# Scores of the first two head pairs taken in row halves of the array from the split halves

## The chip, the cores and the metric

One core of a Trainium2 chip runs the whole program in one launch. The metric is device time in microseconds, the median of several executions; the profile shows one further execution. TensorE (PE) multiplies, with PEld its weight loads; VectorE (DVE), ScalarE (ACT) and GpSimd (POOL) work beside it, and SyncE (SP) issues most DMAs, in the order of its queue. Every engine works through its own instructions in order.

## The reference

Inputs are q, k, v of 2 batches x 8 heads x 768 positions x 64 dimensions, in fp32. Attention is masked by a hash: six projections give six sign bits to each position, and a query sees the keys that have its six bits.

```python
q_bits = (np.einsum('bhsd,dk->bhsk', q, proj) > 0)      # six bits, the same for k
mask = q_bucket[:, :, :, None] == k_bucket[:, :, None, :]
scores = np.where(mask, scale * np.matmul(q, k.transpose(0, 1, 3, 2)), -1e9)
attn = np.exp(scores - np.max(scores, axis=-1, keepdims=True))
attn = attn / (np.sum(attn, axis=-1, keepdims=True) + 1e-09)
return np.matmul(attn, v)
```

The result, 768 x 512 for each batch, goes through a mixture of eight experts with one expert for each token (a gate decides whether a token keeps the expert of the one before it), and then through a second mixing layer over tokens and channels. Both follow the attention, and the change does not touch them.

## The kernel before

The attention walks over eight head pairs (a batch and two neighbouring heads); a pair's q and k lie transposed in one tile `rqk`, with head 0 in partitions 0 to 63 and head 1 in 64 to 127. A **unit** is one head and 128 queries of a pair against all 768 keys, so a pair has 12 units and there are 96; three query blocks of both heads, six units, are a group. The kernel keeps fp32 accuracy with single-pass products: every number is split into a high part (rounded) and a low part (the rest), and the scores are high x high + high x low + low x high. The mask is added by the same matmuls: 12 rows of bits (six signs and their complements, k's scaled by 2^31) add a huge number where a bit differs.

To make three products and the bits with two matmuls of 128 and 76 rows, the parts of a head are first **placed**: `split_hi` and `split_lo` (lines 139 to 162) make the tile `hl` with q high, q low, k high, k low; `place` (L164 to 179) copies them by DMA into `op`, where head h has four operands: q high twice one above the other, k high above k low, q low above q's bits, and k high above k's bits. Pair 0's head 0 is placed by ScalarE, POOL and VectorE at the start instead (L421 to 436). The bits come from `bit_dots` (L109), which uses the array in four column quarters, and `bit_signs`.

Per unit u: `scores` (L187) writes 128 x 768 scores into `ps`, of which there are two; `low` (L202, VectorE, printed at L205) copies them into `sc` and takes their minimum; `expo` (L209, ScalarE) takes the exponential and the sum; `transp` (L215) turns `sc` by six TensorE transposes into two tiles `pst`, evacuates them (two of two on ScalarE for units in `relieve`, otherwise one on ScalarE and one on VectorE), and issues `low` and `expo` of unit u + 2 in between. `av` (L238) multiplies with v, both heads in column halves, one group late; `av_out` and `av_tok` finish a group. The instructions of VectorE's `low` at L205 stand in the order of units, so the n-th of them is that of unit n - 1.

The main loop (L456 on) issues, for each u: `scores(u + 2)`, for odd u of a later group `av`, `transp(u)`, token work of earlier groups, and then what a table `todo` holds for u. That table is filled by `at(u, f)`: the splits and placements of pair n during pair n - 1 (three units later for pair 1), loads of later pairs and of v, bit steps, and single pieces of work for the later layers (`narrow`, errands). So SP's queue holds placements and loads in the order of their units, and each waits for its source.

Of the kernel before, what the change touches and what calls it, by code (L numbers as in the profile page):

```python
# [24 lines left out]
CAP = 256  # L25
OVF = E * CAP
NOV = 64
NW = 4
C_ID, C_TRI, C_ONE = 0, 128, 256
C_CODE, C_M0, C_TOK, C_IOTA, C_W = 128, 136, 142, 154, 410  # L30
THR = -1.5 * 2.0 ** -23
# [22 lines left out]
def warm(nc, cbf, ps, n):  # L54
    for _ in range(n):
        nc.tensor.matmul(ps[:, :384], lhsT=cbf[:, 0:128], rhs=cbf, start=True, stop=True)


def attention(tc, nc, cst, cbf, cst_src, tri_src, cw, qkT, vt, iw_src, route, wide, errands, xh, early):
    with ExitStack() as ctx:  # L60
# [21 lines left out]

        pairs = [(b, p) for b in range(B) for p in range(NP)]
        NPR = len(pairs)
        rawt, vtile, bits, opnd, hls = {}, {}, {}, {}, {}

        def load_pair(i):
            b, p = pairs[i]
            r = raw_p.tile([128, 2, S], F32, name="rqk")
            if i == 0:  # L90
                nc.sync.dma_start(r[:, 1], qkT[b, p, :, 1])
                nc.sync.dma_start(r[:, 0], qkT[b, p, :, 0])
# [39 lines left out]
        def bits_here(s, hf, pd):  # L132
            sl, p = slice(384 * hf, 384 * hf + 384), 64 * s
            to = opnd[0][64:76, 0, 2 + s, sl]
            nc.vector.tensor_scalar(to, pd[p:p + 12, :384], 0.0, cw[p:p + 12, 32:33],
                                    op0=ALU.is_gt, op1=ALU.subtract)
            return to

        def split_hi(i, j):
            raw = rawt[i]  # L140
            if j == 0:
                hls[i] = hl_p.tile([128, 4, S], F32R, name="hl")
                if i == 0:
                    nc.scalar.activation(hls[i][:, 2], raw[:, 1], AF.Copy)
                else:
                    nc.gpsimd.tensor_scalar(hls[i][:, 2], raw[:, 1], 1.0, 0.0, op0=ALU.mult, op1=ALU.add)
            elif i == 0:
                nc.scalar.activation(hls[i][:, 0], raw[:, 0], AF.Copy, scale=-0.125)
            else:
                nc.gpsimd.tensor_scalar(raw[:, 0], raw[:, 0], -0.125, 0.0, op0=ALU.mult, op1=ALU.add)  # L150
                nc.gpsimd.tensor_scalar(hls[i][:, 0], raw[:, 0], 1.0, 0.0, op0=ALU.mult, op1=ALU.add)

        def split_lo(i, j):
            raw, hl = rawt[i], hls[i]
            if j == 0:
                eng = nc.gpsimd if i else nc.vector
                eng.tensor_tensor(hl[:, 3], raw[:, 1], hl[:, 2].bitcast(F32), op=ALU.subtract)
            elif i == 0:
                nc.vector.scalar_tensor_tensor(hl[:, 1], raw[:, 0], -0.125, hl[:, 0].bitcast(F32),
                                               op0=ALU.mult, op1=ALU.subtract)  # L160
            else:
                nc.gpsimd.tensor_tensor(hl[:, 1], raw[:, 0], hl[:, 0].bitcast(F32), op=ALU.subtract)

        def place(i, h, j):  # L164
            if i not in opnd:
# [19 lines left out]
        pss, scs, pts, sums, mns, pav, xTs = {}, {}, {}, {}, {}, {}, {}  # L185

        def scores(u):  # L187
            i, half, qb, h = units[u]
# [26 lines left out]
        def transp(u):  # L215
            _, _, qb, h = units[u]
            g = u // 6
            if u % 6 == 0:
                pts[g] = [pt_p.tile([128, NB, 384], F32, name=f"pt{x}") for x in range(2)]
            sc = scs.pop(u)  # L220
            pt = pts[g][h]
            for n in range(2):
                ps = ps_t.tile([128, 512], F32, name="pst")
                for j in range(3):
                    kb = 3 * n + j
                    nc.tensor.transpose(ps[:, 128 * j:128 * j + 128], sc[:, 128 * kb:128 * kb + 128], ident)  # L226
# [8 lines left out]
            if u + 2 < NU:  # L235
                expo(u + 2)

        def av(g, kb, q0=0, q1=3):  # L238
# [114 lines left out]
        def at(u, f, *args):  # L353
            todo[u].append(lambda: f(*args))

        busy, relieve = set(), set(range(1, NU - 1, 2))
        for n in range(1, NPR):
            u0 = 12 * (n - 1)
            u1 = u0 + 3 if n == 1 else u0
            at(u1, split_hi, n, 0)  # L360
            at(u1, split_hi, n, 1)
            at(u1 + 1, split_lo, n, 0)
            at(u1 + 2, split_lo, n, 1)
            for h in range(2):
                for j in range(4):
                    at(u1 + 3 + j, place, n, h, j)
            if n + 3 < NPR:
                at(u1 + 8, load_pair, n + 3)
            if n + 1 < NPR:
                at(u1 + 8, load_v, n + 1)  # L370
        for u0, ids in ((1, [1]), (9, [2, 3]), (26, [4, 5]), (50, [6, 7])):
            for hf in range(2):
                at(u0 + hf, lambda ids=ids, hf=hf: bit_part(ids, hf, px_tile))
                busy.add(u0 + hf)
# [37 lines left out]
        load_pair(0)  # L412
        nc.sync.dma_start(cst, cst_src)
        load_pair(1)
        idle = ps_a.tile([128, 512], F32, name="pav")
        warm(nc, cbf, idle, 13)
        opnd[0] = op_p.tile([128, 2, 4, S], F32R, name="op")
        op = opnd[0]
        split_hi(0, 0)
        hl = hls[0]  # L420
        split_lo(0, 0)  # L421
        split_hi(0, 1)
        for x in (1, 3):
            nc.gpsimd.tensor_scalar(op[0:64, 0, x], hl[0:64, 2], 1.0, 0.0, op0=ALU.mult, op1=ALU.add)
        pds = [bit_dots([0], hf, pt_tile) for hf in range(2)]
        warm(nc, cbf, idle, 6)
        split_lo(0, 1)
        nc.scalar.activation(op[0:64, 0, 0], hl[0:64, 0], AF.Copy)
        nc.scalar.activation(op[64:128, 0, 1], hl[0:64, 3], AF.Copy)
        nc.scalar.activation(op[64:128, 0, 0], hl[0:64, 0], AF.Copy)  # L430
        nc.scalar.activation(op[0:64, 0, 2], hl[0:64, 1], AF.Copy)
        k0 = bits_here(1, 0, pds[0])
        bits_here(0, 0, pds[0])
        nc.vector.tensor_scalar(k0, k0.bitcast(F32), -MISS, None, op0=ALU.mult)
        k1 = bits_here(1, 1, pds[1])
        nc.vector.tensor_scalar(k1, k1.bitcast(F32), -MISS, None, op0=ALU.mult)
        place(0, 1, 0)
        place(0, 1, 1)
        place(0, 1, 2)
        for hf in range(2):  # L440
            bit_signs(bits[0][0], hf, pds[hf])
        place(0, 1, 3)
        nc.sync.dma_start(op.bitcast(F32)[64:76, 0, 2, 384:], bits[0][0][0:12, 384:])
        nc.sync.dma_start(iw, iw_src)
        nc.sync.dma_start(tri, tri_src)
        load_v(0)
        load_pair(2)
        load_v(1)
        load_pair(3)
        for u in range(2):  # L450
# [5 lines left out]
        for u in range(NU):  # L456
            g, w = u // 6, u % 6
            last = g == NG - 1
            if u + 2 < NU:
# [887 lines left out]
def build(tc, nc, a):  # L1347
    with ExitStack() as ctx:
# [6 lines left out]
        cw = P.tile([128, 33], F32, name="cw")  # L1355
# [75 lines left out]
def arrange(inp):  # L1431
# [1 line left out]

    c = np.ascontiguousarray
    cst, tri = consts()
    cw = np.zeros((128, 33), np.float32)
# [4 lines left out]
    cw[:, 32] = np.where(np.arange(128) < 64, ~first, first)  # L1441
    out = {"cst": cst, "tri": tri, "cw": cw}
    qk = np.stack([inp["q"], inp["k"]], axis=3)
    out["qkT"] = c(np.transpose(qk, (0, 1, 4, 3, 2))).reshape(B, NP, 128, 2, S)
# [28 lines left out]
```

## Time and profile before

| | us |
|---|---|
| median of three runs | 642.21 (639.51 to 643.21) |
| the profiled execution | 639.75 |
| its span, first to last instruction | 637.9 |
| TensorE busy in the span | 621.0 |
| start of the first unit's `low` | 11.60 |
| start of the `low` of unit 24 | 70.52 |

A row of the timeline gives start, length, engine, line, operation, result<-operands, partitions x columns, count; neighbouring instructions of one kind are merged, and the brackets say how long the engine sat idle before and what ended it. The length of a matmul contains its way through the array, so neighbours overlap: a stream's cost is the distance of starts.

### The profile page before, as it was taken

How to read it: one execution, taken by the hardware profiler on the slowest of the kernel's cores; microseconds unless marked ns; L12 is line 12 of the kernel's file. 1: busy time of each engine (PE TensorE's matmuls, PEld its weight loads, DVE VectorE, ACT ScalarE, POOL GpSimd, SP SyncE). 2: the span in 40 equal slices, each digit the busy share in tenths (PEclk: the TensorE clock that was granted, in tenths of full speed). 3: DMA queues.
4: the chain of work that ended last, by engine and by line, in shares of the span. 5: the costliest groups of instructions: out<-in, count | busy, mean ns of one | idle time of the engine just before them, and what ended most of it. 6: DMA issues, size and time to landing. Idle time of an engine off the chain costs nothing. (4 is left out here: it accounts for less than half of the span.)

```text
span 637.9 us, 10353 instructions
## 1 busy us (share of the span) xinstructions
PE 621.0 (97%) x3930; PEld 501.9 (79%) x3930; DVE 404.0 (63%) x743; ACT 355.3 (56%) x645; POOL 262.0 (41%) x195
## 2 busy tenths in 40 slices
PE   7989998999999999999999999999999999999997
PEld 4746766667677677889899889989688887878897
DVE  6636768788888666846885655644356877663352
ACT  5747766767767766454555455444656546743220
POOL 2432221124080241345346354255456766684320
PEclk8979999999999999999999999999999999999999
DMA  7997999965976201688768698764222432221002
GB/s 198 265 234 203 305 260 289 260 165 159 259 219 157 74 1 50 232 294 316 272 226 312 233 308 306 256 247 168 82 85 85 145 100 84 101 97 67 33 34 100
DMA packets 52861, 116.13 MB, mean 182 GB/s; under 512 B 4180, under 2 KB 13664, under 8 KB 52808
## 3 DMA queue, kind: packets, MB, share of 16 engines
q1 hardware_dynamic: 49448, 101.28, 51.2%
q10 hardware_dynamic: 1440, 7.86, 3.6%
q0 software_dynamic: 1920, 6.29, 3.0%
q8 instruction: 32, 0.52, 0.3%
q14 instruction: 21, 0.17, 0.1%
HBM read 74.06 MB, written 22.54 MB: 151 GB/s over the span
## 5 line engine op out<-in xcount | busy, mean ns | idle before, releaser
L205 DVE TENSOR_SCALAR_CACHE_REDUCE sc<-ps 128x768 f32<-128x768 f32 x96 | 91.4, 953 | 33.2 <-PE ps L198 32.2
L1199 PE MATMUL acc<-wt,z 128*128 128x256 f32 (+1 forms) x576 | 105.4, 338 | 0.6 <-DVE z L1185 0.6
L1199 PEld LDWEIGHTS acc<-wt,z 128*128 128x128 f32 x576 | 89.8, 188 | 15.7 <-DVE z L1185 1.5
L784 POOL TENSOR_TENSOR whl<-wr,whl 128x1024 fp32r<-128x1024 f32 x30 | 72.0, 2425 | 69.6 <-ACT whl L782 69.6
L212 ACT ACTIVATE sc<-sc,mn 128x768 f32<-128x768 f32 x96 | 89.8, 936 | 18.6 <-DVE sc L205 15.4
L198 PE MATMUL ps<-op 76*128 76x384 f32 (+1 forms) x384 | 94.2, 367 | 4.8 <-DMA op<-bt 2.2
L857 PE MATMUL mph<-xhl,whl 128*128 128x256 f32 x768 | 94.2, 284 | 0.4 <-DVE xhl L520 0.3
L857 PEld LDWEIGHTS mph<-xhl,whl 128*128 128x128 f32 x768 | 93.2, 192 | 1.3 <-DVE xhl L520 0.5
L226 PEld LDWEIGHTS pst<-cst,sc 128*128 128x128 f32 x576 | 66.5, 143 | 31.7 <-ACT sc L212 18.5
L230 ACT ACTIVATE pt<-pst 128x384 f32<-128x384 f32 x143 | 65.0, 487 | 41.8 <-PE pst L226 41.5
L226 PE MATMUL pst<-cst,sc 128*128 128x128 f32 x576 | 83.6, 282 | 1.7 <-DVE pt L232 1.6
L873 PE MATMUL mpy<-whl,h 128*128 128x512 f32 x336 | 79.5, 392 | 0.0
L198 PEld LDWEIGHTS ps<-op 76*128 76x128 f32 (+1 forms) x384 | 64.5, 194 | 12.9 <-issue 5.9
L243 PE MATMUL pav<-pt,v 128*64 128x384 f32 (+1 forms) x432 | 74.2, 468 | 0.0
L782 ACT ACTIVATE whl<-wr 128x1024 fp32r<-128x1024 f32 x64 | 64.0, 1051 | 15.1 <-PE mpy L873 6.5
L873 PEld LDWEIGHTS mpy<-whl,h 128*128 128x128 f32 x336 | 62.1, 188 | 12.4
L552 POOL TENSOR_TENSOR wt<-wr,wt 128x768 fp32r<-128x768 f32 x24 | 46.2, 1946 | 10.0 <-ACT wt L551 4.6
L243 PEld LDWEIGHTS pav<-pt,v 128*64 128x64 f32 x432 | 26.4, 137 | 28.7 <-issue 28.5
L784 DVE TENSOR_TENSOR whl<-wr,whl 128x1024 fp32r<-128x1024 f32 x34 | 40.0, 1219 | 6.4 <-ACT whl L782 6.4
L860 ACT ACTIVATE h<-mph 128x512 fp32r<-128x512 f32 x32 | 19.1, 596 | 43.1 <-PE mph L857 41.6
L861 DVE SCALAR_TENSOR_TENSOR h<-mph,h 128x512 fp32r<-128x512 f32 x32 | 21.8, 689 | 33.3 <-ACT h L860 33.2
L1225 PE MATMUL bk<-u,wch 128*128 128x512 f32 (+1 forms) x192 | 34.0, 335 | 0.9 <-DVE u L1215 0.9
(186 smaller groups left out, 792.7 us busy)
## 6 DMA issues: line engine op xcount, KB each, us to landing
wr<-w SPq DMA_DIRECT2D x32, 1024.0 KB
op<-hl SPq DMA_DIRECT2D x45, 384.0 KB
wr<-wtf ACTq DMA_DIRECT2D x10, 768.0 KB
w<-wt SPq DMA_DIRECT2D x16, 384.0 KB
rqk<-qkT SPq DMA_DIRECT2D x7, 768.0 KB
xs<-wr SPq DMA_DIRECT2D x8, 512.0 KB
xi<-xs SPq DMA_DIRECT2D x7, 512.0 KB
ys<-y SPq DMA_DIRECT2D x7, 512.0 KB
```

Source lines behind the costliest of these rows:

```text
L198: nc.tensor.matmul(ps[:, n, :384], lhsT=op[:kk, h, x, c0:c0 + 128], rhs=op[:kk, h, x + 1, 384 * n:384 * n + 384], start=(x == 0), stop=(x ...
L205: nc.vector.tensor_scalar(sc.rearrange("p (a b) -> p a b", a=2), pss.pop(u)[:, :, :384], NEG, None, op0=ALU.min, op1=ALU.min, accum_out=mn ...
L212: nc.scalar.activation(sc, sc, AF.Exp, bias=mns[g][:, w:w + 1], scale=-1.0, accum_out=sums[g][:, w:w + 1])
L226: nc.tensor.transpose(ps[:, 128 * j:128 * j + 128], sc[:, 128 * kb:128 * kb + 128], ident)
L230: nc.scalar.activation(dst, src, AF.Copy)
L243: nc.tensor.matmul(pav[g][64 * h:64 * h + 64, sl], lhsT=vtile[g // 2][:, kb, 64 * h:64 * h + 64], rhs=pts[g][h][:, kb, sl], start=(kb == 0 ...
L552: self.nc.gpsimd.tensor_tensor(t[:, 1, r], raw[:, sl], t[:, 0, r].bitcast(F32), op=ALU.subtract)
L782: nc.scalar.activation(t[0][:, sl], raw[:, sl], AF.Copy)
L784: lo.tensor_tensor(t[1][:, sl], raw[:, sl], t[0][:, sl].bitcast(F32), op=ALU.subtract)
L857: nc.tensor.matmul(ps[:, ff], lhsT=w[a][:, w0:w0 + 128], rhs=x[:, bb, k], start=(n == 0), stop=(n == 23))
L873: nc.tensor.matmul(yps[e][n], lhsT=h[:, a, fo, 128 * n:128 * n + 128], rhs=w[bb][:, 512 * f:512 * f + 512], start=(fo == 0 and q == 0), st ...
L1199: nc.tensor.matmul(span(b, d, t0, n), lhsT=z[:, a, r, 128 * d:128 * d + 128], rhs=w[:, bb, r, t0:t0 + n], start=(t == 0 and i == 0 and (d ...
```

## The change

For pairs 0 and 1 (24 units) nothing is placed. `scores2` takes the scores of both heads of one query block in one set of sixteen matmuls, from `hl` where it is: three products, two halves of the keys, two heads, each with 64 rows; head 0 uses rows 0 to 63 of the array and head 1 rows 64 to 127. The bits follow as four matmuls of 12 rows that begin at rows 0, 32, 64 and 96, from tiles that hold every bit row at the place it is used from. It takes both `ps` tiles at once. The loop goes over such sets for the first 22 units; units 22 on run in the old loop. For an odd unit `transp` now issues `low(u + 2)` ahead of its first evacuation and `expo(u + 2)` ahead of its second.

Pair 0's bits are made at their places by three steps with a whole 128-partition result (`first_dots`, `first_signs`); its q is loaded and split in two halves, so that the first set needs only the first. Pair 1's bits are made as before and spread by 12 small DMAs (`second_bits`), eight after unit 5 and four after unit 8; its splits on POOL come after units 0 and 4. The constants, v and the third pair are loaded ahead of the first computing. Six warm-up matmuls go. Both `hl` lie in what was the first operand tile, and the bits in the tile of the expert stage's tokens, which is free then.

```diff
+        def first_dots(x, alloc):
+            pd = alloc()
+            for r in range(4):
+                c, w0 = 32 * r, 12 * (r // 2)
+                rhs = rawt[0][:, 1, HALF[r % 2]] if x == 2 else rawt[0][:, 0, HALF[x]]
+                nc.tensor.matmul(pd[c:c + 32, :384], lhsT=cw[:, w0:w0 + 32], rhs=rhs,
+                                 start=True, stop=True, tile_position=(0, c))
+            return pd
+
+        def first_signs(x, pd):
+            q, k = bbs[0]
+            to, c = (k, 34) if x == 2 else (q[x], 33)
+            nc.vector.tensor_scalar(to, pd[:, :384], 0.0, cw[:, c:c + 1], op0=ALU.is_gt, op1=ALU.subtract)
+            if x == 2:
+                nc.scalar.activation(to, to.bitcast(F32), AF.Copy, scale=-MISS)
...
+        def second_bits(x):
+            bt, r0 = bits[1]
+            q, k = bbs[1]
+            for h in range(2):
+                c = r0 + 12 * h
+                for n in range(2):
+                    r = slice(64 * h + 32 * n, 64 * h + 32 * n + 12)
+                    if x == 0:
+                        nc.sync.dma_start(k.bitcast(F32)[r], bt[64 + c:76 + c, HALF[n]])
+                    nc.sync.dma_start(q[x].bitcast(F32)[r], bt[c:c + 12, HALF[x]])
...
-        units[:6] = sorted(units[:6], key=lambda t: (t[3], t[2]))
...
+        NP2 = 24
+
+        def scores2(p):
+            i, half, qb, _ = units[2 * p]
+            hl, g = hls[i], p // 3
+            q, k = bbs[i]
...
+            ps = [ps_s.tile([128, 2, 512], F32, name="ps") for _ in range(2)]
+            c0 = 384 * half + 128 * qb
+            cols = slice(c0, c0 + 128)
+            for x, (a, bc) in enumerate(((0, 2), (0, 3), (1, 2))):
+                for n in range(2):
+                    for h in range(2):
+                        hs = slice(64 * h, 64 * h + 64)
+                        nc.tensor.matmul(ps[h][:, n, :384], lhsT=hl[hs, a, cols], rhs=hl[hs, bc, HALF[n]],
+                                         start=(x == 0), stop=False)
+            for n in range(2):
+                for h in range(2):
+                    r = slice(64 * h + 32 * n, 64 * h + 32 * n + 12)
+                    nc.tensor.matmul(ps[h][:, n, :384], lhsT=q[half][r, 128 * qb:128 * qb + 128], rhs=k[r],
+                                     start=False, stop=True)
...
+                if u < NP2 - 2 and h == 1:
+                    if n == 0:
+                        low(u + 2)
+                        nc.vector.tensor_copy(dst, src)
+                    else:
+                        expo(u + 2)
+                        nc.scalar.activation(dst, src, AF.Copy)
+                    continue
...
+        busy, relieve = set(), set(range(0, NP2 - 2, 2)) | set(range(NP2 - 1, NU - 1, 2))
         for n in range(1, NPR):
             u0 = 12 * (n - 1)
+            at(u0, split_hi, n, 0)
+            if n == 1:
+                at(u0, split_lo, n, 0)
+                at(u0 + 4, split_hi, n, 1)
+                at(u0 + 4, split_lo, n, 1)
+                at(u0 + 5, second_bits, 0)
+                at(u0 + 8, second_bits, 1)
...
+        nc.scalar.activation(hl[:, 2], rawt[0][:, 1], AF.Copy)
+        first_hi(0)
+        pd = first_dots(2, pt_tile)
+        nc.vector.tensor_tensor(hl[:, 3], rawt[0][:, 1], hl[:, 2].bitcast(F32), op=ALU.subtract)
+        first_signs(2, pd)
+        pd = first_dots(0, pt_tile)
+        first_lo(0)
+        first_signs(0, pd)
+        scores2(0)
+        pd = first_dots(1, px_tile)
         for u in range(2):
-            scores(u)
             low(u)
             expo(u)
+        first_signs(1, pd)
+        at(0, first_hi, 1)
+        at(1, first_lo, 1)
...
+        for p in range(NP2 // 2 - 1):
+            g, w = p // 3, p % 3
+            scores2(p + 1)
+            transp(2 * p)
+            if g >= 1:
+                av(g - 1, 2 * w)
+                av(g - 1, 2 * w + 1)
+                if w == 2:
+                    av_out(g - 1)
+            transp(2 * p + 1)
+            for u in (2 * p, 2 * p + 1):
+                for x in tok.get(u, ()):
+                    av_tok(x)
+                for f in todo.pop(u, ()):
+                    f()
+        for u in range(NP2 - 2, NU):
```

## Rows read from the trace of the kernel before

**Rows 1.** The page: busy time, share of the span and instructions of each engine.

```profile
PE 621.0 (97%) x3930; PEld 501.9 (79%) x3930; DVE 404.0 (63%) x743; ACT 355.3 (56%) x645; POOL 262.0 (41%) x195
```

**Rows 2.** Busy time by stretch; columns: stretch, length, each engine, clock, DMA share, GB/s.

```profile
5.30:12.10 6.80, 4.95 (x32) 2.31 (x30) 6.55 (x10) 4.13 (x6) 3.86 (x4) 1.00 0.96 252
12.10:19.00 6.90, 6.39 (x28) 5.09 (x28) 3.82 (x9) 4.71 (x10) 0.93 (x3) 0.51 0.72 181
39.40:46.30 6.90, 6.90 (x27) 3.12 (x26) 2.95 (x8) 1.97 (x5) 4.26 (x5) 0.51 0.81 241
```

**Rows 3.** TensorE's waits, 70.5 to 637 us, longest first: total, times, longest.

```profile
PE pst L226 <- DVE pt L232: 1.6, 1, 1.6
```

**Rows 4.** The start, in order of time: start us, length us, engine, line, operation.

```profile
5.35 0.96 DVE L157 TENSOR_TENSOR hl<-rqk,hl 128x768 fp32r<-128x768 f32 x1 [4.10 <-ACT hl L144]
5.53 1.50 PE L118 MATMUL pst<-rqk,cw 128*32 128x384 f32 x16
11.60 0.95 DVE L205 TENSOR_SCALAR_CACHE_REDUCE sc<-ps 128x768 f32<-128x768 f32 x1
12.47 0.95 DVE L205 TENSOR_SCALAR_CACHE_REDUCE sc<-ps 128x768 f32<-128x768 f32 x1
```

**Rows 5.** The timeline around pair 1's first unit.

```profile
34.67 0.85 PE L118 MATMUL px<-rqk,cw 128*32 128x384 f32 x8
35.65 0.62 DVE L125 TENSOR_SCALAR bt<-px,cw 128x384 f32<-128x384 f32 x1 [2.06 <-issue]
38.31 0.30 PEld L198 LDWEIGHTS ps<-op 76*128 76x128 f32 x2 [2.56 <-DMA op<-bt]
39.52 1.51 PE L118 MATMUL px<-rqk,cw 128*32 128x384 f32 x8
```

**Rows 6.** The timeline of one round with `av`; narrow windows split some merged rows.

```profile
53.69 1.51 PE L243 MATMUL pav<-pt,v 128*64 128x384 f32 x8
54.39 0.82 PE L243 MATMUL pav<-pt,v 128*64 128x384 f32 x4
54.71 0.49 PE L243 MATMUL pav<-pt,v 128*64 128x384 f32 x2
55.13 0.88 PE L226 MATMUL pst<-cst,sc 128*128 128x128 f32 x6
55.76 0.95 PE L198 MATMUL ps<-op 128*128 128x384 f32 x4
56.38 0.34 PE L198 MATMUL ps<-op 76*128 76x384 f32 x1
56.55 0.82 PE L226 MATMUL pst<-cst,sc 128*128 128x128 f32 x6
56.84 0.96 DVE L205 TENSOR_SCALAR_CACHE_REDUCE sc<-ps 128x768 f32<-128x768 f32 x1 [1.98 <-PE ps L198]
57.13 0.95 PE L198 MATMUL ps<-op 128*128 128x384 f32 x4
58.01 1.51 PE L243 MATMUL pav<-pt,v 128*64 128x384 f32 x8
```

**Rows 7.** The timeline: `low` of units 5, 8, 9 and 24.

```profile
22.71 0.96 DVE L205 TENSOR_SCALAR_CACHE_REDUCE sc<-ps 128x768 f32<-128x768 f32 x1 [0.32 <-PE ps L198]
26.95 0.96 DVE L205 TENSOR_SCALAR_CACHE_REDUCE sc<-ps 128x768 f32<-128x768 f32 x1 [0.56 <-ACT pt L230]
28.31 0.96 DVE L205 TENSOR_SCALAR_CACHE_REDUCE sc<-ps 128x768 f32<-128x768 f32 x1
70.52 0.96 DVE L205 TENSOR_SCALAR_CACHE_REDUCE sc<-ps 128x768 f32<-128x768 f32 x1 [0.56 <-PE ps L198]
```

**Rows 8.** The timeline: one bit DMA's issue; first and last step of pair 1's split.

```profile
13.54 0.72 SPq L443 DMA_DIRECT2D op<-bt  x1
23.07 0.83 POOL L146 TENSOR_SCALAR hl<-rqk 128x768 fp32r<-128x768 f32 x1
27.37 1.84 POOL L162 TENSOR_TENSOR hl<-rqk,hl 128x768 fp32r<-128x768 f32 x1
```

More of the change, by code (lines that the diff above doesn't have):

```diff
@@ L28 @@
 NW = 4
+HALF = slice(0, 384), slice(384, 768)
 C_ID, C_TRI, C_ONE = 0, 128, 256
@@ L84, in attention @@
         NPR = len(pairs)
-        rawt, vtile, bits, opnd, hls = {}, {}, {}, {}, {}
+        rawt, vtile, bits, bbs, opnd, hls = {}, {}, {}, {}, {}, {}
         def load_pair(i):
@@ L91, in load_pair @@
                 nc.sync.dma_start(r[:, 1], qkT[b, p, :, 1])
-                nc.sync.dma_start(r[:, 0], qkT[b, p, :, 0])
+                for x in range(2):
+                    nc.sync.dma_start(r[:, 0, HALF[x]], qkT[b, p, :, 0, HALF[x]])
             else:
@@ L141, in split_hi @@
             if j == 0:
[L142 to L148, printed above, removed]
+                if i not in hls:
+                    hls[i] = hl_p.tile([128, 4, S], F32R, name="hl")
+                nc.gpsimd.tensor_scalar(hls[i][:, 2], raw[:, 1], 1.0, 0.0, op0=ALU.mult, op1=ALU.add)
             else:
@@ L154, in split_lo @@
             raw, hl = rawt[i], hls[i]
[L155 to L162, printed above, removed]
+            nc.gpsimd.tensor_tensor(hl[:, 3 - 2 * j], raw[:, 1 - j], hl[:, 2 - 2 * j].bitcast(F32), op=ALU.subtract)
         def place(i, h, j):
@@ L185, in attention @@
         pss, scs, pts, sums, mns, pav, xTs = {}, {}, {}, {}, {}, {}, {}
+        NP2 = 24
[3 more added lines that the diff above has]
+            q, k = bbs[i]
+            if p % 3 == 0:
+                sums[g] = sm_p.tile([128, 6], F32, name="sum")
+                mns[g] = sm_p.tile([128, 6], F32, name="mn")
+            ps = [ps_s.tile([128, 2, 512], F32, name="ps") for _ in range(2)]
[12 more added lines that the diff above has]
+                                     start=False, stop=True)
+            for h in range(2):
+                pss[2 * p + h] = ps[h]
         def scores(u):
@@ L234, in transp @@
                     low(u + 2)
-            if u + 2 < NU:
+            if u + 2 < NU and (u >= NP2 - 2 or h == 0):
                 expo(u + 2)
@@ L354, in at @@
             todo[u].append(lambda: f(*args))
-        busy, relieve = set(), set(range(1, NU - 1, 2))
+        busy, relieve = set(), set(range(0, NP2 - 2, 2)) | set(range(NP2 - 1, NU - 1, 2))
         for n in range(1, NPR):
             u0 = 12 * (n - 1)
[L359 to L366, printed above, removed]
+            at(u0, split_hi, n, 0)
[5 more added lines that the diff above has]
+                at(u0 + 8, second_bits, 1)
+            else:
+                at(u0, split_hi, n, 1)
+                at(u0 + 1, split_lo, n, 0)
+                at(u0 + 2, split_lo, n, 1)
+                for h in range(2):
+                    for j in range(4):
+                        at(u0 + 3 + j, place, n, h, j)
             if n + 3 < NPR:
-                at(u1 + 8, load_pair, n + 3)
+                at(u0 + 8, load_pair, n + 3)
             if n + 1 < NPR:
-                at(u1 + 8, load_v, n + 1)
-        for u0, ids in ((1, [1]), (9, [2, 3]), (26, [4, 5]), (50, [6, 7])):
+                at(u0 + 8, load_v, n + 1)
+        for u0, d, ids in ((1, 2, [1]), (9, 2, [2, 3]), (26, 1, [4, 5]), (50, 1, [6, 7])):
             for hf in range(2):
-                at(u0 + hf, lambda ids=ids, hf=hf: bit_part(ids, hf, px_tile))
-                busy.add(u0 + hf)
+                at(u0 + d * hf, lambda ids=ids, hf=hf: bit_part(ids, hf, px_tile))
+                busy.add(u0 + d * hf)
         free = [u for u in range(16, NU) if u % 6 != 1 and u not in busy]
@@ L414, in attention @@
         load_pair(1)
[L415 to L444, printed above, removed]
         nc.sync.dma_start(tri, tri_src)
@@ L447, in attention @@
         load_pair(2)
+        nc.sync.dma_start(iw, iw_src)
         load_v(1)
         load_pair(3)
+        idle = ps_a.tile([128, 512], F32, name="pav")
+        warm(nc, cbf, idle, 13)
+        t = op_p.tile([128, 2, 4, S], F32R, name="op")
+        hls[0], hls[1] = t[:, 0], t[:, 1]
+        t = xh.tile([128, 2, 4, CAP], F32R, name="xhl").rearrange("p a d t -> p (a d t)")
+        part = [t[:, 384 * x:384 * x + 384] for x in range(5)]
+        bbs[0], bbs[1] = (part[0:2], part[2]), ((part[4], part[0]), part[3])
+        hl = hls[0]
+        nc.scalar.activation(hl[:, 2], rawt[0][:, 1], AF.Copy)
[8 more added lines that the diff above has]
+        pd = first_dots(1, px_tile)
         for u in range(2):
-            scores(u)
             low(u)
             expo(u)
+        first_signs(1, pd)
+        at(0, first_hi, 1)
+        at(1, first_lo, 1)
         nc.gpsimd.tensor_copy(cbf[:, 0:128], ident)
         nc.gpsimd.tensor_copy(cbf[:, 128:384], tri)
-        for u in range(NU):
+        for p in range(NP2 // 2 - 1):
[14 more added lines that the diff above has]
+        for u in range(NP2 - 2, NU):
             g, w = u // 6, u % 6
@@ L1354, in build @@
         half_pi = P.tile([128, 2], F32, name="hpi")
-        cw = P.tile([128, 33], F32, name="cw")
+        cw = P.tile([128, 44], F32, name="cw")
         nc.sync.dma_start(cw, a["cw"])
@@ L1441, in arrange @@
     cw[:, 32] = np.where(np.arange(128) < 64, ~first, first)
+    cw[:, 33], cw[:, 34] = ~first, first
     out = {"cst": cst, "tri": tri, "cw": cw}
```

14 lines of the change are left out of this document (7 added, 7 removed).

## The prediction

> **What bounds the kernel now.** First the page's busy times [rows 1]: TensorE is busy for 97% of the span, VectorE 63%, ScalarE 56%. Then the table by stretches [rows 2]: in the attention the granted clock was 0.51 of 2.4 GHz, its lower level, from 12.1 to 19.0 and from 39.4 to 46.3 us, and 1.00 before the first. Ahead of the first TensorE was busy for only 4.95 of 6.80 us; ahead of the second it sat waiting 2.56 us for bit rows of the placed operands [rows 5]. Then who TensorE waited for from 70.5 us on [rows 3]: longest 1.6 us for VectorE, and none of the 13 causes that the view lists is a DMA. So what the first units gain or lose on TensorE is passed on to the end, and DMA traffic that goes away saves nothing by itself. I therefore follow one mark, the start of unit 24's `low` (the first unit behind the change), at 70.52 us [rows 7]. The code behind it is the same in both kernels.
>
> **The start.** Before, `low(0)` starts at 11.60 us [rows 4], behind ScalarE's and POOL's operand copies and VectorE's 12-partition steps. After, the split of the k half is the same and ends at 5.35 + 0.96 = 6.31 [rows 4]. The bit matmuls start at 5.53 [rows 4]; eight take 0.85 [rows 5], so the k dots are there at 6.4 and their signs (0.62, [rows 5]) at 7.0. The low part of half of q has 384 columns: between 0.48 (half of that subtraction) and 0.96; I take 0.6, nearest the half, so 7.6, and q's signs end at 8.25. ScalarE's casts, the scaling of k's bits and the first eight score matmuls fit beside that. The closing matmuls need 0.15 + 0.34 + 0.12 us (change of shape, latency and hand-over, worked out below): `low(0)` at 8.9, 2.7 us earlier.
>
> **What a set of scores for two units costs TensorE.** Now a block of four score matmuls takes 55.76 to 56.55 = 0.79; the last of it holds the array for 56.38 to 56.55 = 0.17, so the first costs 0.11 more [rows 6]. Two units take two blocks. After, a set has sixteen matmuls: twelve of 64 rows, which can go two at once, and four of 12 rows in four row groups. No row shows row halves side by side. Column halves are shown: two `av` matmuls lie within one 0.49 us stretch, a pair starts 0.32 after the other (54.39, 54.71) [rows 6], and eight matmuls of 32 columns end within 0.85 [rows 5]. Bounds: all side by side, 6 + 1 slots, 7 x 0.17 + 0.11 = 1.30; none, 16 slots, 2.83. I take 1.30, since the column rows are the nearest.
>
> What the set adds are changes of the array's shape. Around `av` two are visible [rows 6]: the block ahead of it takes 57.13 to 58.01 = 0.88 instead of 0.79 (+0.09), 53.69 to 55.13 = 1.44 where four pairs at 0.32 are 1.28 (+0.16), and six transposes behind it 0.63 (55.13 to 55.76) instead of 0.58 (56.55 to 57.13; +0.05). Together 0.30, or 0.15 a change. The set has three: to halves, to quarters, back. Bounds for each: 0, as a block's step from 128 to 76 rows costs nothing (its last matmuls are no slower than 0.17), and 0.30, all of it in one change. I take 0.15, nearest `av`: 0.45 a set.
>
> The Trainium skill, "TensorEngine Tiling (Array Packing)", Key Properties, says that changing the tiling mode, and not just the tile, drains the engine. By that rule all three changes pay and the 0.45 stands; by the row of the step from 128 to 76 rows alone they would be free and the result 4.4 us lower. I follow the rule, because `av`'s changes do pay, 0.15 each.
>
> **Rounds without `av`** (a round is a pair of units). A set writes both score buffers, and each comes free only with its `low`, so the two `low` no longer overlap the next set. Round: two `low` back to back 0.87 + 0.95 [rows 4], hand-over 0.12 (56.38 + 0.34 to 56.84 [rows 6]), set 1.30, two changes 0.30, and from the slot of the last matmul to the next `low` 0.46 - 0.17 = 0.29. Sum 3.83. Before, two units took (28.31 - 22.71) / 2 = 2.80 [rows 7]. Four such rounds lead to `low(8)`: 15.3. The clock: I assume one low stretch like that at 12.1 again, as TensorE's start stays broken. In it TensorE bounds the round: (1.30 + 2 x 0.58) x 2 + 0.45 = 5.4. The 6.9 us hold 1.3 such rounds, 1.3 x 1.6 = 2.1, and a bit step of 0.85 that is no longer hidden: 2.9. So `low(8)` at 8.9 + 15.3 + 2.9 = 27.1; it was at 26.95 [rows 7]. The start's gain is gone by here.
>
> **From `low(8)` to `low(24)`**, rounds with `av`. Before: 70.52 - 26.95 = 43.6, in which lie 16 blocks, the wait of 2.56 and the low clock behind it: 6.9 us at half speed, 3.4 lost (bit matmuls 1.51 for 0.85 [rows 5]). After, seven sets and one block: 7 x 1.75 + 0.79 = 13.0 against 16 x 0.79 = 12.6, 0.4 worse. `low` no longer decides: 1.82 + 0.4 us are less than the 2.65 of transposes and `av` between two sets (0.58 + 1.44 + 0.63). All else, bits and token steps too, is in both.
>
> The wait and its low clock, 6.0 together, go: pair 1 is no longer placed. POOL's splits of it (five steps, 23.07 to 29.21 [rows 8], 6.1 us) come in two portions, and twelve small bit DMAs are left. Each costs SP about 0.72, as the one of 18 KB before [rows 8]: the first eight from some 23 us, when the second bit step's signs are done, to 29; landed by 32 if they take the 2.56 that TensorE waited before. Pair 1's first closing matmul is at about 36: 4 us of slack. SP reaches them behind pair 3's load, whose buffer is free when pair 0's last split is done, at some 16 us; behind them stand the loads of later pairs, which have 20 us and more. Pair 2's placements keep their units and POOL reaches its split some 4 us sooner: no new wait. ScalarE still evacuates three transposed tiles of four, in another order: nothing. The extra q load is half a microsecond of issue beside the warm-up matmuls: nothing, or 0.4 if the k half were behind it.
>
> So `low(24)` at 27.1 + 43.6 - 6.0 + 0.4 = 65.1.
>
> **Sum.** 70.5 - 65.1 = 5.4: +2.7 (start) + 6.0 (wait and clock) - 3.3 (first rounds, sets). The profiled execution took 639.75 us, 637.9 of them span; by its own time that gives 634.3. It lay 2.5 under the median of the runs shown, 642.21; against that the forecast is **636.8 us**. Its own range by the change of shape: 29 changes on the path (4 x 2 + 7 x 3), at 0 4.4 lower, 632.4; at 0.30 4.4 higher, 641.2.
>
> **Rivals.**
> - A second low stretch in the first rounds. For: TensorE idles for about 0.9 of 3.8 us in each, and both low stretches followed a TensorE with gaps [rows 2, 5]. Against: each gap is a third of the 2.56 ahead of 39.4. Price 2.1 to 3.4, say 2.7: 639.5.
> - No low stretch at the start, as more bit matmuls and a set lie in it: 633.9.
> - Weight loads. Each of the sixteen matmuls needs its own, and a transpose with its load takes 0.10 (six in 0.58 [rows 6]). If the loads of two halves go one after the other, a slot is 0.20 and the four small ones 0.40: 1.6 for 1.19, x 11 sets = 4.5, or 6 with the clock: 641.3 to 643, no change. Against: the eight 32-column matmuls' loads do not show it.
> - Pair 1's bits are late after all; the 6.0 come back: 642.8.
> - Slower: row halves go in single file. A set is 16 slots, 1.53 more, x 11 = 16.8: 653.6. Its place is the 64-row score matmuls; from 0.49 more a set on, the gain is eaten, and from 0.78 on the kernel is measurably slower. In this case the change doesn't do what it says.
>
> The Trainium skill, "TensorE: Matmul & The Clock Gate", Part 3, Measured speedup vs the span model, gives 3.07x for four row tiles; no run here shows it. By it the last rival is false, and the four small matmuls take 0.22 instead of 0.17, 0.6 us in all.
>
> **How the numbers follow.** Chances: forecast 0.45, second low stretch 0.22, no low stretch 0.10, weight loads 0.09, late bits 0.07, single file 0.07. The range, 632.0 to 644.5, takes in the bounds of the changes, the clock both ways and the two rivals near 642; it leaves out the last rival and the tails. 0.5% of the median, about what a measurement here can tell, is 3.2 us: faster is under 639.0. That holds some four fifths of the forecast's own cases, two fifths of the second stretch's and all of the third's: 0.53. Slower, over 645.4, is single file and the tails of late bits, weight loads and what I have not thought of: 0.14. The rest, 0.33, is no change.
>
> **What would show it.** `low(0)` at about 8.9; in the first rounds at full clock two `low` back to back, 3.8 between pairs, TensorE waiting for them; 64-row matmuls starting in twos, a pair per 0.17; gaps of 0.15 at the changes; no DMA wait at pair 1's first set; clock 1.00 around 40 us; `low(24)` near 65. Wrong would be a set of over 1.8 us, halves in single file, a second low stretch, or a span that does not end earlier by what `low(24)` gained.

## The result, and the profile after

The changed kernel took 634.03 us (median of 4 runs, 633.27 to 636.94), the kernel before 641.01 beside it: ratio 0.990, 95% interval 0.985 to 0.994. Run twice more on other occasions it gave 0.992 (0.989 to 0.995) and 0.992 (0.990 to 0.995). The forecast was 636.8, a gain of 5.4 us; by these ratios 5 to 7 us came. The profiled execution is the slowest of the four, 636.94 us with a span of 635.1; where it lost time is told below.

The page's busy times, then the table by stretches that answers to [rows 2] (stretch, length, each engine, clock, DMA share, GB/s):

```profile
PE 620.9 (98%) x4028; PEld 498.2 (78%) x4028; DVE 402.7 (63%) x740; ACT 351.4 (55%) x643; POOL 256.8 (40%) x191
```

```profile
5.30:12.10 6.80, 6.08 (x57) 2.98 (x50) 4.86 (x9) 3.00 (x7) 1.90 (x4) 1.00 1.01 336
12.10:19.00 6.90, 6.39 (x60) 3.99 (x56) 5.73 (x12) 5.44 (x13) 1.96 (x2) 1.00 0.47 126
39.40:46.30 6.90, 6.90 (x58) 4.68 (x54) 4.60 (x8) 3.18 (x8) 6.70 (x7) 1.00 0.50 116
```

TensorE is busy for as long as before [rows 1], but the clock no longer falls at 12.1 and 39.4 us. In the 6.80 us ahead of 12.1 TensorE is busy for 6.08 us where it was 4.95. Its waits from 10 to 68 us (total, times, longest) name no DMA, where before there was the 2.56 of [rows 5]:

```profile
PE pst L270 <- ACT pt L282: 0.8, 3, 0.3
PE ps L221 <- DVE sc L249: 0.7, 2, 0.4
```

The timeline of the start (answers to [rows 4]) and of the first rounds (to [rows 7]). L139 and L120 are bit matmuls, L221 the 64-row and L226 the 12-row score matmuls, L249 `low`; the tiles print as `op` and `xhl` because `hl` and the bits lie in those:

```profile
5.15 1.50 PE L139 MATMUL pst<-rqk,cw 128*32 128x384 f32 x16
5.44 0.96 DVE L490 TENSOR_TENSOR op<-rqk,op 128x768 fp32r<-128x768 f32 x1 [4.19 <-ACT op L487]
...
7.31 0.61 DVE L146 TENSOR_SCALAR xhl<-pst,cw 128x384 fp32r<-128x384 f32 x1
8.07 0.45 PE L226 MATMUL ps<-xhl 12*128 12x384 f32 x4
...
8.56 0.96 DVE L249 TENSOR_SCALAR_CACHE_REDUCE sc<-ps 128x768 f32<-128x768 f32 x1 [0.64 <-PE ps L226]
9.44 0.95 DVE L249 TENSOR_SCALAR_CACHE_REDUCE sc<-ps 128x768 f32<-128x768 f32 x1
...
14.06 0.85 PE L120 MATMUL px<-rqk,cw 128*32 128x384 f32 x8
14.85 0.44 PE L221 MATMUL ps<-op 64*128 64x384 f32 x2
...
24.73 0.96 DVE L249 TENSOR_SCALAR_CACHE_REDUCE sc<-ps 128x768 f32<-128x768 f32 x1 [1.43 <-PE ps L226]
```

`low(0)` is at 8.56 instead of 11.60, `low(8)` at 24.73 instead of 26.95. The bit step at 14.06 stands ahead of a set that is already due. One round with `av` (answers to [rows 6]; the last row is cut by the window):

```profile
25.34 1.51 PE L295 MATMUL pav<-pt,v 128*64 128x384 f32 x8
26.78 0.87 PE L270 MATMUL pst<-cst,sc 128*128 128x128 f32 x6
27.59 1.32 PE L221 MATMUL ps<-op 64*128 64x384 f32 x12
28.83 0.45 PE L226 MATMUL ps<-xhl 12*128 12x384 f32 x4
29.21 0.87 PE L270 MATMUL pst<-cst,sc 128*128 128x128 f32 x6
30.01 0.54 PE L295 MATMUL pav<-pt,v 128*64 128x384 f32 x2
```

A set takes 27.59 to 29.21 = 1.62; from `av` to `av` it is 4.67, where before it was 53.69 to 58.01 = 4.32. Twelve 64-row matmuls fit into the 1.24 ahead of the 12-row ones (one at a time they would be twelve slots, each the 0.17 us for which a matmul of 384 columns holds the array: 2.1), so they go two at a time, and the four small ones, with the change behind them, take 0.38.

At the end of the changed part VectorE misleads. The scores of unit 24 start at 63.27, 6.2 us earlier than before (69.44), but `low(24)` only 4.6 earlier (70.52). The timeline of before, then of the changed kernel:

```profile
69.44 0.95 PE L198 MATMUL ps<-op 128*128 128x384 f32 x4
```

```profile
61.59 3.61 POOL L181 TENSOR_TENSOR hl<-rqk,hl 128x768 fp32r<-128x768 f32 x2
63.27 0.95 PE L242 MATMUL ps<-op 128*128 128x384 f32 x4
63.69 1.72 DVE L592 TENSOR_SCALAR w<-w 128x384 uint32<-128x384 uint32 x1
65.92 0.95 DVE L249 TENSOR_SCALAR_CACHE_REDUCE sc<-ps 128x768 f32<-128x768 f32 x1
```

VectorE was held in L592 beside POOL's subtraction (what such holds are is told at the end). TensorE did not wait for it, so the mark that I had chosen is 1.6 late and TensorE's own row is the one to follow. The lead then grew to 7.5 us, mostly because the 1.6 of [rows 3] fell away (at unit 36), and between units 70 and 72 it shrank to 3.1 at one place:

```profile
173.09 0.87 PE L270 MATMUL pst<-cst,sc 128*128 128x128 f32 x6
173.72 0.94 PE L242 MATMUL ps<-op 128*128 128x384 f32 x4
175.62 0.49 ACT L282 ACTIVATE pt<-pst 128x384 f32<-128x384 f32 x1 [3.10 <-PE ps L242]
176.16 0.55 PE L270 MATMUL pst<-cst,sc 128*128 128x128 f32 x3 [1.51 <-ACT pt L282]
```

ScalarE stands 3.10 us although the transposes that it copies ended at 173.96; the clock is low from 178.7 to 182.2. The releaser that the row names, the score matmuls of L242, ended at 174.66, and the copy does not read them; the cause stays open. The stretch from `low(68)` to `low(74)` takes 19.1 us here and 15.2 in the profile of before; eight of the fourteen profiled executions, of variants of both kernels, have 19 or more. So these two profiles, set side by side, show less than the medians do. In the third run's profile the clock is 1.00 to the end, the span 632.6 (before: 637.9), the lows of units 60 to 95 5.9 us earlier than before.

### The profile page after: what moved, and what is told of

It is laid out like the page before. It is cut to its first block, busy times and chain, and to the rows that moved or that the text cites. A ratio compares the mean times of both kernels' runs of the same rounds, so it can differ in the third digit from the quotient of the medians.

```text
span 635.1 us, 10543 instructions
## 1 busy us (share of the span) xinstructions
PE 620.9 (98%) x4028; PEld 498.2 (78%) x4028; DVE 402.7 (63%) x740; ACT 351.4 (55%) x643; POOL 256.8 (40%) x191
## 5 line engine op out<-in xcount | busy, mean ns | idle before, releaser
L249 DVE TENSOR_SCALAR_CACHE_REDUCE sc<-ps 128x768 f32<-128x768 f32 x96 | 90.7, 953 | 29.1 <-PE ps L242 14.5
L270 PEld LDWEIGHTS pst<-cst,sc 128*128 128x128 f32 x576 | 64.1, 141 | 35.4 <-ACT sc L256 14.4
L282 ACT ACTIVATE pt<-pst 128x384 f32<-128x384 f32 x132 | 59.6, 488 | 51.1 <-PE pst L270 47.8
L242 PE MATMUL ps<-op 128*128 128x384 f32 (+1 forms) x288 | 68.6, 360 | 0.5 <-DVE sc L249 0.5
L242 PEld LDWEIGHTS ps<-op 128*128 128x128 f32 (+1 forms) x288 | 47.2, 190 | 3.5 <-issue 2.5
L924 ACT ACTIVATE h<-mph 128x512 fp32r<-128x512 f32 x32 | 19.1, 596 | 42.6 <-PE mph L921 41.1
```

The source lines that it names most:

```text
L242: nc.tensor.matmul(ps[:, n, :384], lhsT=op[:kk, h, x, c0:c0 + 128], rhs=op[:kk, h, x + 1, 384 * n:384 * n + 384], start=(x == 0), stop=(x ...
L249: nc.vector.tensor_scalar(sc.rearrange("p (a b) -> p a b", a=2), pss.pop(u)[:, :, :384], NEG, None, op0=ALU.min, op1=ALU.min, accum_out=mn ...
```

## The experiments

All were timed in five rounds beside the kernel before. Those on the changed kernel are held against its own ratios, 0.990 to 0.992; beside the runs on single file, on shape and on VectorE's steps it was not timed itself. My theory: the gain is the start plus the removed wait and its low clock, less dearer sets.

**Is the second pair's wait one for its bits?** The kernel before, bit placements first:

```diff
-                for j in range(4):
-                    at(u1 + 3 + j, place, n, h, j)
+                for x, j in enumerate((3, 0, 1, 2) if n == 1 else range(4)):
+                    at(u1 + 3 + x, place, n, h, j)
```

> The kernel before, with one change: of pair 1's placements the bit rows are copied first and not last. Theory (the wait for pair 1's bits and the low clock behind it were the largest single loss, and the change gains by taking them away): TensorE doesn't wait at 35.8 us, the clock stays at its upper level around 40 us, and 2.5 + 3.4 = 5.9 us go: about 635, nearly the time of the changed kernel, without any row halves. First rival (the wait moves to the operand that is now last, the low parts): 0 to -2.5, 639 to 641. Second rival (the low clock comes by itself and not from the wait): -2.5, 638.5.

639.17 us, ratio 0.999 (0.997 to 1.002). In time and in the wait it is the first rival: the wait moved to the operand that is now placed last. The timeline:

```profile
36.49 1.52 PE L198 MATMUL ps<-op 128*128 128x384 f32 x4 [2.19 <-DMA op<-hl]
```

The profiled execution is the fastest of the twelve, 636.57, and its low clock is shorter at both places, from 12.8 to 16.2 and from 36.7 to 40.1; so its `low(14)`, 3.0 us earlier than before, need not stand for the others.

**Is the low clock at the start due to TensorE's gaps?** The kernel before, with warm-up matmuls in them:

```diff
+                    if u == 0 and (x, n) in ((0, 1), (2, 0)):
+                        warm(nc, cbf, idle, 4)
...
+        warm(nc, cbf, idle, 6)
```

> The kernel before, with fourteen more warm-up matmuls put into the gaps of TensorE's start, between 8.9 and 12.6 us; their result is not used. Theory (the low clock from 12.1 to 19.0 follows from a start of TensorE with gaps; in the changed kernel it is absent because that stretch is filled better): the low stretch at 12.1 goes and 2.8 us with it, about 638; the one at 39.4 stays, or moves with the wait. Rival (the clock falls there whatever TensorE does): 641, or up to 0.7 us worse if the extra matmuls stand in the way.

640.87 us, ratio 1.001 (0.999 to 1.003). The low stretch at 12 us went: TensorE was busy for 6.23 of the 6.80 us ahead of it (4.95 before), clock 1.00, and `low(6)` came 1.86 us earlier. One profile is weak evidence, for with the start unaltered the low stretch there was 3.4 us long in two other runs' profiles and absent in one (5.08 and 5.18 us busy ahead, and 5.68). But the twelve executions point the same way: their mean clock has a median of 0.9945, that of the kernel before beside them 0.989, and one stretch of 6.8 us at half speed is 0.005 of the span. In the time nothing of it arrived. The timeline:

```profile
35.78 0.59 PE L198 MATMUL ps<-op 128*128 128x384 f32 x2 [2.12 <-DMA op<-hl]
38.15 1.01 PE L198 MATMUL ps<-op 76*128 76x384 f32 x2 [1.77 <-DMA op<-bt]
```

The last operands of the second pair's first set were there at 38.15, before at 38.31; the wait had grown. So the terms of my sum are not independent: an earlier start is worth something only where the placement behind it does not stay.

**What is the wait worth if it goes?** The kernel before, the second pair split and placed three units earlier (the loads behind it stay at their units):

```diff
-            u1 = u0 + 3 if n == 1 else u0
+            u1 = u0
...
```

> The kernel before with the second pair split and placed three units earlier, nothing else. The earlier run that only changed the order of the placements left the wait where it was, on the last operand placed, so the wait of 2.56 us and the low clock behind it (3.4 us in the trace of before) were never taken away. Theory (that wait and what follows it are 6 us of the profiled time, more than half of the whole gain): the wait is gone, the clock stays at 1.00 from 16 us on, and the time is 3 to 6 us under the kernel before, 634 to 637 us. Rival (TensorE only waits for something else there, POOL's splits or the bit rows, or the low clock comes anyway): within 1.5 us of the kernel before, 639 to 641 us.

POOL now scales the second pair's queries before the bit matmuls read them, so those bits come out inverted; the work is the same. 641.27 us, ratio 0.999 (0.996 to 1.001): in time the rival, though by two effects that cancel. TensorE's waits, 20 to 60 us:

```profile
PE px L118 <- POOL rqk L150: 2.8, 1, 2.8
```

The bit matmuls wait for that scaling, the clock is low from 19.3 to 26.1 us behind it, and `low(11)` is 4.27 us late. So TensorE comes late to the second pair's first set and finds its operands there:

```profile
39.72 0.97 PE L198 MATMUL ps<-op 128*128 128x384 f32 x4
```

From unit 11 to 14, without the wait and at clock 1.00, 5.64 us are won back: `low(14)` is 1.37 early. That is the 6.0 of my sum, seen by itself. The run does not show that the operands came sooner.

The same with the queries scaled behind the bit matmuls, placed two units earlier:

```diff
-            at(u1, split_hi, n, 0)
-            at(u1, split_hi, n, 1)
+            x = 3 if n == 1 else 0
+            at(u0, split_hi, n, 0)
+            at(u0 + x, split_hi, n, 1)
...
-                    at(u1 + 3 + j, place, n, h, j)
+                    at(u0 + 3 + x // 3 + j, place, n, h, j)
```

> The kernel before with the second pair split and placed earlier, as in the run before it, but the queries are scaled and split only at unit 3, after the bit products that read them, so that no bit product waits for POOL; placement at units 4 to 7 (two earlier than before). Theory (the wait on the second pair's placement and the low clock behind it cost 5.6 us, the difference that the run before showed between units 11 and 14): the start of the low of unit 14 comes 4.5 to 6 us before that of the kernel before, 41.5 to 43.0 us where that has 47.5, and the time is 4 to 6 us lower. Rival (the low stretches belong to the first 45 us as a whole, whichever wait is taken away): the clock falls at another place there, the low of unit 14 comes less than 3 us earlier, and the time is within 2 us of the kernel before.

638.55 us, ratio 1.001 (0.999 to 1.003): the rival. The low stretch at 12 us is absent in this profile, that at 38 stayed, and the wait grew to 5.2 us:

```profile
37.13 0.59 PE L198 MATMUL ps<-op 128*128 128x384 f32 x2 [3.39 <-DMA op<-bt]
39.50 1.01 PE L198 MATMUL ps<-op 76*128 76x384 f32 x2 [1.78 <-DMA op<-bt]
```

Issued earlier (the last bit rows by 32.2 us, before by 35.8), the transfers did not land earlier (39.50, before 38.31). The table by stretches, 18 to 39 us, of the kernel before, of this one and of the changed one in its third run:

```profile
18.00:39.00 21.00, 18.76 (x128) 12.90 (x128) 11.19 (x23) 13.99 (x31) 7.73 (x9) 0.98 0.94 247
```

```profile
18.00:39.00 21.00, 16.33 (x113) 11.53 (x111) 10.84 (x23) 12.86 (x30) 7.90 (x9) 0.97 1.03 263
```

```profile
18.00:39.00 21.00, 20.75 (x170) 12.58 (x171) 12.25 (x28) 14.87 (x34) 4.54 (x5) 1.00 0.41 141
```

The DMA engines' share is 0.94 and 1.03 with the placement, 0.41 without. Three edits of order or time left the second pair's first set between 36.5 and 39.5 us; the change takes 2.3 MB out of that stretch. The run with the bits inverted fits in: SP's last load behind the placements waited for one of them until 37.6 us there and 39.0 here, with issues about 1 us apart.

**Are transfers that nobody awaits worth anything?** The changed kernel with six 384 KB placements into a buffer that nothing reads:

```diff
...
+                for h in range(2):
+                    for j in range(3):
+                        at(u0 + 6 + j, place_unread, n, h, j)
```

> The changed kernel with six transfers of 384 KB put back that place the second pair's parts into a buffer that nothing reads, at the units 6 to 8. Theory (the gain comes from what TensorE no longer waits for, the transfers themselves cost it nothing): the changed kernel's time, 634 us, within 1 us. Rival (part of the gain is that the DMA queues and the transfers that others wait for are relieved): 636 to 640 us, with a DMA wait in front of TensorE between 20 and 60 us.

638.68 us, ratio 0.995 (0.993 to 0.997); the changed kernel beside it 638.22, 0.992 (0.989 to 0.995). The theory holds within the noise: 0.5 us apart by the medians, and the intervals overlap. In the trace `low` is 0.2 late up to unit 23, some 1.5 from unit 28 on; TensorE waits 0.4 for the third pair's bits and 1.1 for a held `low`:

```profile
64.31 0.59 PE L257 MATMUL ps<-op 76*128 76x384 f32 x2 [0.42 <-DMA op<-bt]
```

So of the gain 0.4 is shown to be such relief, and 1.5 is the most that this trace allows. The 1.1 is of the kind that differs between two runs of one kernel (last section).

**Control**, the changed kernel in two of these groups:

> The changed kernel itself, unaltered, as the measure for the others of this group. Both theories: about 634 us, 0.99 of the kernel before. Where its profile loses 2.3 to 4 us at one place between units 69 and 72 (about 175 to 182 us), as every profile of an altered kernel so far does, the loss belongs to the profiled execution; its starts of the lows from unit 53 to 69 should again be 7.3 to 7.7 us ahead of the kernel before.

638.22 us, 0.992. Up to unit 69 the lows are 8.4 us ahead of before (expected 7.3 to 7.7); then the stop described above.

> The changed kernel unaltered, as the measure for this group: 634 to 638 us, 0.99 of the kernel before; granted clock 1.00 over the first 170 us.

633.21 us, 0.992; clock 1.00, as expected.

**Row halves only for the first pair**, the second split at unit 0 and placed at units 2 to 5:

```diff
-        NP2 = 24
+        NP2 = 12
...
+                for h in range(2):
+                    for x, j in enumerate((0, 1, 3, 2)):
+                        at(u0 + 2 + x, place, n, h, j)
...
```

> The changed kernel with only the first pair in row halves: the second pair is split at unit 0 and placed at units 2 to 5, three units earlier than in the kernel before. Theory (the gain is the start and the absent wait on the second pair's placement, and each of its six rounds with av in row halves costs 4.67 us where 4.32 was paid on placed operands): six times 0.36 = 2.1 us are saved where the operands are there in time, 632 us, no DMA wait longer than 0.3 us at the second pair's first set. Rival (the transfers of the placement can't be finished by the time that the faster start now asks for them): TensorE waits 2 to 3 us for the second pair's operands and the clock falls behind it, 637 to 640 us.

(Here too the second pair's query bits come out inverted.) 640.94 us, ratio 0.999 (0.996 to 1.001), over 2 us worse than the control beside it: in time the rival. The profiled execution, the fastest of the twelve, shows how close it is:

```profile
35.95 0.44 PE L242 MATMUL ps<-op 128*128 128x384 f32 x1 [0.37 <-DMA op<-hl]
```

There the wait is 0.37 and the rounds behind it win back what the start lost: TensorE's scores of unit 24 start at 62.94, in the control at 63.11. (`low(24)` is 1.9 us earlier, but the control's is held as described above.) The other executions' mean clock goes down to 0.988 (control: 0.995 to 1.00), so a longer wait with its low clock is likely there; their traces were not taken.

**Do the halves run side by side?** The changed kernel, one head's six matmuls behind the other's:

```diff
-            for x, (a, bc) in enumerate(((0, 2), (0, 3), (1, 2))):
+            for h, x, a, bc in ((h, *t) for h in range(2) for t in ((0, 0, 2), (1, 0, 3), (2, 1, 2))):
...
```

> The changed kernel, with the twelve 64-row matmuls of a set ordered head 0 first and then head 1, so that no two neighbours lie in different row halves. Theory (halves run side by side only when neighbours alternate, and a set costs 1.2 us of TensorE for that reason): six slots of 0.175 more, 1.05 us a set; seven sets of the rounds with av count in full, 7.4 us; in the four rounds without av head 0's low can start early, so there 0 to 2 us: 641 to 643 in all. Rival (TensorE is not what bounds these rounds, or the halves run one by one already): 634.

641.54 us, ratio 1.002 (1.000 to 1.004): in time the theory. The timeline:

```profile
25.25 1.78 PE L220 MATMUL ps<-op 64*128 64x384 f32 x12
26.96 0.45 PE L225 MATMUL ps<-xhl 12*128 12x384 f32 x4
```

1.71 us in place of 1.24, 0.47 a set where I had 1.05. TensorE's scores of unit 24 start at 69.29, 6.0 later than in the changed kernel: nearly the whole gain rests on the halves going in twos. It isn't the single file that the prediction's rival priced: twelve slots of 0.17 would be 2.1, so part of the second head's matmuls still ran beside the first's.

**What does a change of shape cost?** The changed kernel, two changes more in a set (the 12-row matmuls ahead of the last product):

> The changed kernel, with the four 12-row matmuls of a set moved between the second and the third product, so that a set has five changes of the array's shape and not three. Theory (each change costs 0.09 to 0.28 us, as the gaps between matmuls in the changed kernel's trace show): 0.2 to 0.45 us more a set, times 11 sets, 2 to 5 us: 636 to 639. Rival (what a set loses at its ends is waiting for other engines, and a change of shape is free): 634.

638.17 us, ratio 0.996 (0.994 to 0.998): the theory. The timeline of a set:

```profile
28.96 0.97 PE L221 MATMUL ps<-op 64*128 64x384 f32 x8
29.86 0.45 PE L227 MATMUL ps<-xhl 12*128 12x384 f32 x4
30.23 0.61 PE L221 MATMUL ps<-op 64*128 64x384 f32 x4
30.77 0.87 PE L271 MATMUL pst<-cst,sc 128*128 128x128 f32 x6
```

A set is 1.81 instead of 1.62: 0.1 for each added change, 2.1 us over eleven sets; TensorE's scores of unit 24 start 2.7 later. That a change of the tiling mode drains the engine (the Trainium skill, "TensorEngine Tiling (Array Packing)", Key Properties) agrees with these rows.

**One change fewer:** `av` ahead of the first transposes:

```diff
-            transp(2 * p)
             if g >= 1:
                 av(g - 1, 2 * w)
...
+            transp(2 * p)
             transp(2 * p + 1)
```

> The changed kernel with the two av steps of a round between the scores and the first transposes, where they stood between the two units' transposes: four changes of the array's shape in a round instead of five. Theory (every change of shape costs TensorE 0.1 to 0.3 us, nothing else limits such a round): a round with av takes 4.3 to 4.5 us instead of 4.67, TensorE's scores of unit 24 start 1.5 to 3 us earlier (near 61 us), the time is 1 to 3 us below the changed kernel. Rival (av stood there to cover the copies out of the two transposition buffers; without it TensorE waits for ScalarE's and VectorE's copies in each round): the round stays at 4.6 us or grows, waits of transposes on copies of over 0.3 us in each round, the same time or slower.

637.21 us, ratio 0.999 (0.997 to 1.000), 4.0 above the control: the rival. The timeline, from `av` to `av`:

```profile
24.52 1.51 PE L295 MATMUL pav<-pt,v 128*64 128x384 f32 x8
25.96 0.88 PE L270 MATMUL pst<-cst,sc 128*128 128x128 f32 x6
27.09 0.93 PE L270 MATMUL pst<-cst,sc 128*128 128x128 f32 x6 [0.25 <-ACT pt L282]
...
29.61 1.51 PE L295 MATMUL pav<-pt,v 128*64 128x384 f32 x8
```

5.09 instead of 4.67: `av` between the transposes covers ScalarE's copy. Such waits, 0.25 each, come eleven times up to 70 us, where the third run has three.

**Keep VectorE's steps away from POOL's subtractions?**

```diff
-        free = [u for u in range(16, NU) if u % 6 != 1 and u not in busy]
+        free = [u for u in range(16, NU) if u % 12 in (3, 4, 5, 6, 8, 9) and u not in busy]
+        free = sorted(free + [u for u in free if u % 12 in (5, 8)])
```

> The changed kernel with VectorE's steps that narrow the weights (three a block, 128x384 integers) kept out of the five units around each pair's first, in which POOL subtracts the low parts; two steps are put into one unit at some others, and the last is at unit 90 instead of 77. In the runs of the changed kernel those steps took 0.35 us alone and up to 2.1 us beside POOL's subtraction, and VectorE's excess over its fastest steps came to 11 to 16 us between 40 and 235 us. Theory (that excess reaches TensorE where the low of a unit stands behind a held step, and makes the changed kernel's gain wander between 5.5 and 8.4 us from run to run): no narrowing step over 1.2 us before 240 us, excess of VectorE under 6 us, the kernel 1 to 2.5 us faster than the changed one, 0.986 to 0.990 of the kernel before. Rival (TensorE's margin of two units swallows nearly all of it): no step held, but the time as of the changed kernel, 0.990 to 0.993.

642.30 us, ratio 1.003 (1.000 to 1.005): both were wrong. The steps were still held (17 us beyond the fastest steps of their kind; POOL's subtractions, behind DMAs, run at other times than their units say). TensorE waited for VectorE for 3.6 us between 70 and 160 us, in the third run of the changed kernel for 1.4; that two steps in one unit are the cause is not shown. It says nothing on the theory.

## Why the prediction was right

Right in the total and in what carries it (the start, the absent wait, the halves in twos). That the total is so near is partly luck: it holds two errors of opposite sign, about 2.0 us in the first rounds and 1.2 in the sets.

- The start: 3.0 us earlier for 2.7 predicted; signs, halves and closing matmuls came in the order that I had worked out.
- First rounds: without bit steps they took 3.63 and 3.76 us where I had 3.83. **The step that failed** is the assumed low stretch, 2.9 us: it did not come. My rival without it (chance 0.10) happened: bit matmuls and a set keep TensorE busy for 6.08 of the 6.80 us ahead, and the clock stays at 1.00 there in all nine profiles of the changed kernel and its variants; filling the gaps of the kernel before did the same. In its place two bit steps lie on TensorE's path without the low clock (14.06 to 14.85, rounds of 4.47 and 4.31). From `low(0)` to `low(8)` it was 16.2 us for 18.2 predicted, so `low(8)` is at 24.73, not 27.1.
- Sets: 16 matmuls in 1.24 + 0.38 as 6 + 1 slots and changes; a slot of 0.17 is right. Changes were too small: a round with `av` is 0.35 dearer than before, I had 0.17. By the starts of the single matmuls, beyond steps within one shape, those into halves take 0.28, to 12 rows 0.09, back to transposes 0.26: 0.63 where I had 0.56 (three changes and the 0.11 of the first matmul). The step from transposes to `av` takes 0.17 where that from a block took 0.09. Seven such rounds cost 2.4 us where 0.17 gives 1.2 (the 0.4 of my sum has one block less after than before).
- The wait and its low clock: 6.0 predicted, 5.64 seen alone. From the first `av` to the ninth, TensorE won 28.11 - 25.34 = 2.8 to 71.68 - 65.50 = 6.2, so 3.4 more; 5.64 - 2.4 gives 3.2.
- Pair 1's bits: SP issued them from 17.25 to 28.4, 0.71 to 0.94 each, and TensorE never waited for them. The rivals on a second low stretch, weight loads and single file did not come.
- "DMA traffic that goes away saves nothing by itself" held where it was tried: with six transfers of the same size put back that nobody awaits, the time stayed within 0.5 us. But I drew it from the waits behind 70.5 us and missed what the traffic does to a transfer that is awaited: from 18 to 39 us the DMA engines were busy for 0.94 of the time, and an earlier issue did not make the operands land earlier.

In sum TensorE's lead at unit 24 is 6.2 us for 5.4 predicted.

## What to carry to other kernels

Before adding up gains ahead of a wait on a transfer, ask whether the transfer would come sooner: here two runs came up to 1.9 us earlier to it, and in both the wait took most or all of that back; only doing without these transfers let the gains through, and it was not being rid of the bytes that counted but not having to wait for them. Small array tiles pay if neighbours alternate between row groups and changes of shape stay few, each being 0.1 to 0.3 us. Whatever fills a gap of TensorE ahead of the steady state may also keep its clock, so a forecast should price that from the gaps of the new order, not carry the old stretch over.

## What the hardware showed unexpectedly

A VectorE step can stand for as long as POOL's. The timeline of the kernel before:

```profile
94.78 1.84 POOL L157 TENSOR_TENSOR hl<-rqk,hl 128x768 fp32r<-128x768 f32 x1
95.00 1.67 DVE L271 TENSOR_TENSOR L<-L,lg 128x27 f32<-128x27 f32 x1
```

27 elements take 0.19 us elsewhere; here 1.67, and the end comes 0.05 after POOL's (96.67, 96.62). The Trainium skill, "SBUF — State Buffer", SBUF: two separate sides, says that of a GpSimd instruction and a VectorE one with two SBUF inputs whichever starts first holds a shared pair of ports for its whole instruction; this agrees. What VectorE's steps take beyond the fastest of their kind, counted where it is over 0.2 us, sums to 9 to 17 us between 40 and 235 us of each profile, mostly beside TensorE's path; how much of it is such holds is not separated. Where a `low` or a copy stands behind one, TensorE loses 0.8 to 1.8 us, and which runs do differs: the lead of the changed kernel at unit 60 was 7.5, 8.3 and 5.8 us in its three profiles.
